# A gated attention and Mish block on one core: TensorE products on tiles of 64x32 in two fixed sets, with halves linked through SyncE

## The chip, the core and the metric

The kernel runs on one core of a Trainium2 chip. Five engines work side by side, each on its own queue in order: TensorE (PE in the profile; its weight loads are listed as PEld), VectorE (DVE), ScalarE (ACT), GpSimd (POOL) and SyncE (SP), which here issues nearly all DMAs. They wait for each other through semaphores. The metric is the device time of one execution in microseconds; the kernel before took 746.05 us (median of three runs, 746.04 to 746.26).

## What is computed

`x` is 2048 tokens of 640 channels in bf16. Two branches are mixed by a gate of one number per token:

```python
g = sigmoid((x * gate_w).sum(-1, keepdims=True))
qkv = x @ wqkv                                  # 32 heads of 20 channels
p = softmax(q @ k.T * 20 ** -0.5)               # 32 x 2048 x 2048
a = (p @ v) @ wo
h = x @ w1 + b1                                 # 1536 channels
b = (h * tanh(softplus(h))) @ w2                # Mish
out = g * a + (1 - g) * b
```

The bulk is the exponential of 32 x 2048 x 2048 scores, which have to leave PSUM (TensorE's output memory, 8 banks of 128 x 512 f32) through ACT or DVE.

## The kernel before

**Attention.** The heads are taken four at a time (8 quads p), the queries 512 at a time (4 chunks c), in 32 groups of 64 score units (`uinfo`, line 396). A unit is one head, one block of 128 keys and 512 queries: one matmul of 32 rows (20 channels, zero padded) by 128 keys, on one of four row strips of the array (`emit_score`, line 933), into one PSUM bank. Up to four units of different heads are issued together and use the four strips at once. Seven banks (`NBANK`) hold scores and every other product; the eighth (`ACCB`) holds the attention output of the current group.

**Exponential.** A unit is read either by ACT (line 1312, one instruction for one, two or three adjacent banks) into a ring of 34 bf16 buffers `E`, or by DVE (line 1347), which writes the bits of a bf16 number by a multiply and an add in integers. To make that piecewise-linear exponential good, three shifted copies of it are summed: two more copies are made from the first with an integer add by POOL or DVE (line 1365, two units per instruction). So an ACT unit is one operand for the product with the values and a DVE unit is three.

**Values.** The product with V takes 128 keys by 32 columns per matmul, on one of four column strips (`emit_pv`, line 1000): four heads run at once and add up in bank `ACCB`. DVE copies the finished group out (line 1406); the softmax denominator, which a column of ones in V delivers, makes a round trip through DRAM over SP's queue (`acc_out`, lines 1592 to 1631), and POOL multiplies.

**The rest of TensorE's work** is cut in pieces of one contraction step each ("misc" units: projections of q, k and v, the dense layer and its second product, the output projection). Each piece is four matmuls of 128 rows by 32 columns on the four column strips (`mm4`, line 512).

**Order.** Python code (`make_plan`, line 422) walks through a clock with costs, and decides what each engine's next instruction is: `poll_pe` (line 1156) prefers scores, then value products, then misc pieces by due times. A constant `ORDER` (line 124) then gives the order in which the planned steps are put into the program. PE takes its queue in that order; an instruction that waits holds everything behind it. Between matmuls on row strips (32x128) and matmuls on column strips (128x32) the plan charges 111 ns (`pe_run`, line 893).

```python
    def emit_score(n, bk):
        g, p, c, kt, r = uinfo(n)
...
                K.kT[32 * r : 32 * r + 32, p % 3, kt * P : (kt + 1) * P],
                K.qT[32 * r : 32 * r + 32, p % 3, c * QC : (c + 1) * QC],
...
                (32 * r, 0),
```

Of the kernel before, what the change touches and what calls it, by code (L numbers as in the profile page):

```python
# [11 lines left out]
P = 128  # L12
ACT = mybir.ActivationFunctionType
ALU = mybir.AluOpType
# [9 lines left out]
VS = 22  # L24
# [28 lines left out]
for _c in range(NQC):  # L53
# [5 lines left out]
PAR = {  # L59
    "thr": 311.432865850951,  # L60
    "lead": 183.56579879480037,
    "dvw": 38.53743660585776,
    "gpmax": 3438.021927551807,
    "xmin": 2062.5527122350004,
    "xwait": 370.8568233744456,
    "urgent": 22.685657497992203,
    "kq": 2.9970653505716234,
    "v0": 30.539278203984722,
    "slack": 141.97275980676932,
    "fill": 0.64,  # L70
# [5 lines left out]
    "wl": 6.4206626210236575,  # L76
    "last": 2.936423220458476,
    "mb": 9,
    "elow": 20.682307524088536,
    "ahd": 5.108513768085364,  # L80
    "age": 6.220859528764049,
    "eres": 0.018977235113313735,
    "vk": 3,
    "a3": 7,
    "a3gp": 1688.8815596232141,
    "hold": 6,
    "idlek": 7,
    "swait": 155.25662470383708,
    "flush": 8,
    "tailh": 0,  # L90
    "dahead": 387.7453029112783,
    "mgb": 0.0,
    "xb": 3.0,
    "ph": 591.0767712730124,
    "wp": 37.52540751652794,
    "wo": 23.808422394577885,
    "thr_2": 337.7597040015291,
    "lead_2": 105.70712187325442,
    "gpmax_2": 6725.390524273934,
    "xmin_2": 3714.088827176782,  # L100
    "xwait_2": 515.3394389040967,
    "vk_2": 3.0,
    "a3gp_2": 2139.6517249172894,
    "dahead_2": 194.37405724273543,
    "age_2": 10.493975161462359,
    "ahd_2": 3.0816465538756317,
    "hold_2": 4.0,
    "idlek_2": 4.0,
    "mb_2": 8.0,
    "dvw_2": 36.65964931310165,  # L110
    "slack_2": 120.90571614233303,
    "mgb_2": 0.0,
# [4 lines left out]
for _k in ("thr", "lead", "gpmax", "xmin", "xwait", "vk", "a3gp", "dahead", "age", "ahd", "hold", "idlek", "mb", "dvw", "slack", "mgb", "xb"):  # L117
# [6 lines left out]
ORDER = (  # L124
    "007000000000000000000000000000000000000000005000000000000000000000000000000000000000000000000000000000000000000000000000001000"
    "000000000000000000000000000001000000002001000000000000000000000000001000000000000000000000001000000000000001000000000000001000"
    "000000000000000000000000000000000001000000000000000000000000000001000000000000000000000000000000000000000000000000000000000000"
    "000000000000000000000000000000000000000000000000000000000000000000000000001000000000000000000000000000000000000000000000000000"
    "000001000000000000000000000000000000000000000000000001000000000000000000001002000000001002000000000000000000000000000001000000"
    "000000000000000000000000000000000000000000000000000000000000000000000000000000000000000000000000000000000000000001004005006007"  # L130
    "00900800a00000000a00b00000000000000000100300000000d00000400100200300500600700800a00e009000002000002001000001000000003004006002"
    "00500700800000900b00a00c00d00e00800f01001301401601501201701901801101b01c01e01d01f00000600800700900a00b00c00d00e00f010016014013"
    "01201501a00000800a00000500000a00000200000200000000d000001003002000002001000000003001000004003000006001000006002003005007001000"
    "00500000200500b00000200000200400000600500700200900a00800d00c00b01000e01301101601201501701800f01901b01a01d01c01e01f020021023024"
    "02202502702802a02902c02f02e02b03003703503403303103a03603803903b02d03c03d04003f041042032044053000033032031000022023025027024029"
    "02802a02b02c02e02f03003103203303403803700002101d02302202402502602702802d02a03003102c00002402d02a03002e029031026039033032034035"
    "03600002e02f03403503203703603803903300002a02d02c03002e02f02103303103503a03403203c00002002102200000e01001400000100600500800400b"
    "00700c00300e00a00901001200d00f01501101300000300400500600800700900b00a00c00d00e01201001100001401101201301501901601b00000a01200b"
    "01301100f00000700800000600800900b00a00700d00c00e01001100f01201500000300400000500000400500900e00301000000500600800000000200000c"
    "00300600500b00e00a00900800700f01c01101001201301401601701501901801b01d01f01a01e00001401301a01901801501b016017000000000000000000"  # L140
    "00000100300700500800000a00c00800900b00400000d00b00c00f00500000400800000300000400300e00800900600a00700b01600d01000f011000000001"
    "00000000300200700600900000800900000a00500300600000700000300600100a00200800400f000005002007009000008000000000000001000000000000"
    "00500200000000100000100200000000100000200100000000100000100000100000100000000600100800400000900100a00500800c00300701001300b000"
    "00100000000000000200300900600a00b00c00d00e00101001101301401500000301300101501601b01701400e00401801901a01201c000012013000000001"
    "00300600800000c00800500200a00b00701001100d00e01401500f01301601701801a01201c01d01902702001b02202402301f02502802601e02a02102c02d"
    "02e03002f03202903403503703303803603a03b03c03102b03e03f03904104004404604504704804a04c04e04204d03d04f04905105204b043054053057056"
    "05005905505800005905805a05c05705d06305f06005b06205e06506106406706806a06606906d06c06f06e07007207107507707607307807d07a07c07f079"
    "08208106b08008408508308708807b08a08908b08608e09008d09209409308c08f07409609500009609109409209307809509c09809909a09d0970a309b000"
    "01701300000600500c00000f00700900a00601100801600d01201300c01701801000101f01501b01a01401c02401e02000001400000800a00c00d00e00f000"
    "00c000000000000000001008000000000005003002001006000003002006001004000003004000000000000000000000001000006009001005008002004007"  # L150
    "00d00c00b00e01100a01201301401900f00001300000700800000600700500800900b00a00d00e00c000001000002000003002004006009005019007000002"
    "00400600500300800900700d00a00e00f01401200000100800a00b00c00f00501000e00d00000300800200100500700600d00900f00a01000c00000700e00a"
    "00d01000f012011013000003000000000002001000000001000000000001000000000000000000001000000000000000000000000000000000000000002001"
    "00000100000000000100300400600000300600000000100400200300000000300100200400600a00800c00900500b00d00000b00700800d00a000003005007"
    "006000000002001000000000000000000000001002005003004000001000001000002001003000004000005002004006007000007000002001000000001000"
    "00000000000100200300500400a00900800700d00c00e00600f01101201001601401501701801a01e01b01301c01d02002301f02201902100001901c01a01e"
    "01d02001f02300000600701400900a00c00d00f00e01000b01600000200800100400000400300500100600900700a008000000002006003001005007008009"
    "00a00e00b00c00d01000f01101701201301601901801a01b00001b01a00000800900c00f01100e00d010000012011015016014013017018000000000000000"
    "00100200500400300600700d00c00b01100e00801000f01201301401601501b01702001a01801c01f01d01e02101902302400902502202602802702902c02b"
    "02d02e03002f03103302a00002a02b02e02d03003203303102c00000c00e00f00d01101001301400000e01301100000700b00c00a00501000400d000000001"  # L160
    "00000000000100300500000200600800700500900b00a00c00e00f01000d01201101501401601800001501601700000900000800700a00900600c00b00d010"
    "00f00e01100000000200000000200100300000100000200b00000200300500400700600800e00d00b00c00f00901101201501301401601701901801b01a01d"
    "01c02102001e01f02302502202602400001801701901c01b01e01d02200000500600700902c00a00d00c01400000400600500300800700a00b00c01300e00d"
    "01001401201101500000700000000000100000100300200f00500700001d00500600701000900002300602500002200d00400500e01002d00000100000601b"
    "00200901c00b00100001200700a00001e00700900601602d00b02302401801701902601b02502803402902a02b00c00a01d02c03a01203002e01f02f03c022"
    "02000002900702b01f00000001b00001701501801d01601c01a01e01f02102302202002402602802502700001801902001a01c01d01e01f021022023025024"
    "00000f00c00d00e01001101601201301401501701b01c01901a01802501d01f02302002202602401e02802102702902a02f02b03402e03102c02d030032036"
    "03803503304003c03a03904403b03d03e00003403b03703803a03c04103d02c04204000000e00800d01201301101601700901501400f010000000005001004"
# [85 lines left out]
    "00000b00000500700200900600000900a000000000004005000000002000000000"  # L254
)


class Names:
    pass


def unpack(text):

    lo, out = 0, set()
# [1541 lines left out]
```

## Time and profile before

| | |
|---|---|
| time, median of three runs | 746.05 us |
| the profiled execution, first to last instruction | 745.1 us |
| what lies around it | 0.95 us |
| TensorE clock granted | 1.000 |
| first score starts / last score starts | 10.4 us / 731.7 us |
| ACT: first exponential starts | 10.87 us |
| PE: matmuls, each with a weight load | 10,332 |
| score units read by ACT / by DVE | 1,464 / 584 |

How to read the profile: its page gives the busy time of each engine (matmuls are pipelined and their ends are modelled, so "busy" on PE is not PE at its peak), then the chain of work that ended last, then groups of like instructions, with busy time, mean duration of one, and the idle time just before them with what ended it. A group's mean duration contains the latency of an instruction (an ACT exponential of two banks lasts 1,060 ns but the next one starts 904 ns after it), so what an engine can carry is read from start to start.

### The profile page before, as it was taken

Reading aid. Unit: us, or ns where it says so; the run is one execution under the profiler, and the core shown is the slowest. Engines: PE = TensorE matmul, PEld = TensorE weight load, DVE = VectorE, ACT = ScalarE, POOL = GpSimd, SP = SyncE. Lnnn points to the kernel's source line nnn. Section 1 sums busy time; section 2 is a strip of 40 time slices with the busy share of each in tenths; the row PEclk is TensorE's granted clock in tenths of the full one; section 3 lists DMA queues with packets and bytes.
Section 4 is the critical chain, followed back from the end, with each engine's and each line's share of the span. In section 5 each row is a group of like instructions: output and inputs, shape, how many; then the busy total and the mean of one; then the engine's idle time right before and its main releaser. Section 6 shows DMA issues by size and latency. Waiting matters only on the chain.

```text
span 745.1 us, 24873 instructions
## 1 busy us (share of the span) xinstructions
PE 729.6 (98%) x10332; PEld 255.2 (34%) x10332; DVE 607.1 (81%) x1047; ACT 713.2 (96%) x750; POOL 521.9 (70%) x501
## 2 busy tenths in 40 slices
PE   8999999999999999999999999999999999999997
PEld 4433343333235333333332222223433333333333
DVE  4688888888979797988788878887878788797876
ACT  6899989999999999999999999999999999999995
POOL 9466735565578557667676587687986788797884
PEclk9999999999999999999999999999999999999999
DMA  9611120011011000112102211130111111211202
GB/s 284 199 48 54 50 82 17 20 52 39 17 29 60 16 29 26 50 44 74 39 28 59 54 43 50 39 101 21 43 52 39 39 38 39 71 60 60 72 21 86
DMA packets 45720, 41.82 MB, mean 56 GB/s; under 512 B 20120, under 2 KB 39240, under 8 KB 45608
## 3 DMA queue, kind: packets, MB, share of 16 engines
q1 hardware_dynamic: 42984, 39.94, 17.8%
q8 instruction: 80, 1.31, 0.7%
q10 hardware_dynamic: 2624, 0.31, 0.3%
q14 instruction: 32, 0.26, 0.1%
HBM read 27.59 MB, written 12.38 MB: 54 GB/s over the span
## 4 chain that ended last, share of the span: by engine, by line
PE 80%; ACT 10%; DVE 7%; issue 2%; POOL 0%; DVEq 0%; ACTq 0%; POOLq 0%
PE ps L507 80%; ACT E L1312 9%; DVE E L1347 4%; DVE E L1365 2%; DVE accs L1406 0%; POOL E L1365 0%; ACT act L1236 0%; PE ps L1753 0%; PE ps L520 0%; ACT xT L528 0%; ACT L1236 0%; DVE bst L656 0%; DVEq L1801 0%; DVE qT L544 0%; DVE ost L689 0%
## 5 line engine op out<-in xcount | busy, mean ns | idle before, releaser
L1312 ACT ACTIVATE E<-ps 128x1024 bf16<-128x1024 f32 (+2 forms) x723 | 680.0, 1070 | 19.3 <-PE ps L507 16.4
L1365 POOL TENSOR_SCALAR E<-E 128x1024 uint16<-128x1024 uint16 x431 | 457.8, 1063 | 209.7 <-DVE E L1347 155.0
L1347 DVE TENSOR_SCALAR E<-ps 128x512 uint16<-128x512 f32 x584 | 388.8, 684 | 94.1 <-PE ps L507 85.6
L507 PE MATMUL ps<-E,VA 128*32 128x512 bf16 x3216 | 299.4, 383 | 1.7 <-DVE E L1347 0.6
L507 PE MATMUL ps<-qT,kT 32*128 32x512 bf16 x2048 | 284.0, 384 | 5.3 <-ACT E L1312 2.6
L507 PEld LDWEIGHTS <-kT 32*128 32x128 bf16 x2048 | 75.3, 91 | 261.3 <-issue 257.2
L507 PEld LDWEIGHTS <-VA 128*32 128x32 bf16 x3216 | 78.9, 95 | 97.5 <-issue 78.2
L1365 DVE TENSOR_SCALAR E<-E 128x1024 uint16<-128x1024 uint16 x153 | 97.9, 643 | 2.0
L507 PE MATMUL ps<-R,act 128*32 128x320 bf16 x1536 | 87.1, 302 | 0.4 <-ACT act L1236 0.4
L507 PE MATMUL ps<-xT,R 128*32 128x512 bf16 x960 | 82.4, 383 | 0.0
L507 PEld LDWEIGHTS <-R 128*32 128x32 bf16 (+1 forms) x1728 | 40.8, 95 | 44.7 <-issue 34.0
L507 PEld LDWEIGHTS <-act 128*32 128x32 bf16 x1536 | 36.4, 95 | 32.1 <-issue 22.2
L637 DVE TENSOR_SCALAR act<-ps,b1f 128x512 bf16<-128x512 f32 x48 | 35.7, 744 | 7.4 <-PE ps L507 6.6
L507 PE MATMUL ps<-wv,xT 128*32 128x241 bf16 (+2 forms) x720 | 37.6, 276 | 0.5 <-DVE E L1347 0.3
L507 PE MATMUL ps<-wk,R 128*32 128x320 bf16 (+1 forms) x640 | 37.5, 303 | 0.2
L507 PE MATMUL ps<-xT,wq 128*32 128x512 bf16 x400 | 34.8, 383 | 0.1
L507 PE MATMUL ps<-xT,wk 128*32 128x512 bf16 (+1 forms) x360 | 34.7, 384 | 0.0
L1620 POOL TENSOR_TENSOR ons<-accs,rb 128x512 bf16<-128x512 f32 x24 | 31.5, 1310 | 1.8 <-DVE E L1347 0.7
L567 DVE CAST stg<-ps 128x512 bf16<-128x512 f32 (+1 forms) x40 | 27.3, 683 | 5.1 <-PE ps L507 4.9
L507 PEld LDWEIGHTS <-xT 128*32 128x32 bf16 (+1 forms) x720 | 19.6, 96 | 13.0 <-issue 9.4
L1406 DVE COPY accs<-ps 128x512 f32<-128x512 f32 x31 | 21.2, 684 | 1.3 <-PE ps L507 1.0
L1236 ACT ACTIVATE act<-act 128x3072 bf16<-128x3072 bf16 x8 | 21.5, 2752 | 0.0
(72 smaller groups left out, 190.3 us busy)
## 6 DMA issues: line engine op xcount, KB each, us to landing
rb<-rd_d SPq DMA_DIRECT2D x124, 64.0 KB
qd<-stg SPq DMA_DIRECT2D x20, 128.0 KB
b_d<-bst SPq DMA_DIRECT2D x16, 160.0 KB
out_dram<-ost SPq DMA_DIRECT2D x16, 160.0 KB
kT<-kd SPq DMA_DIRECT2D x28, 80.0 KB
qT<-qd SPq DMA_DIRECT2D x28, 80.0 KB
stg<-b_d SPq DMA_DIRECT2D x13, 160.0 KB
kd<-stg SPq DMA_DIRECT2D x16, 128.0 KB
```

The costliest lines, as they stand in the source:

```text
L507: K.nc.tensor.matmul(o, lhsT=l, rhs=r, start=first, stop=last, tile_position=pos, skip_group_check=True)
L567: K.nc.vector.tensor_copy(out=K.stg[0:w, s, :], in_=bank(b)[0:w, :])
L637: K.nc.vector.tensor_scalar(out=K.act[:, f, (c % 2) * QC : (c % 2 + 1) * QC], in0=bank(b), scalar1=K.b1f[:, f : f + 1], scalar2=None, op0= ...
L1236: K.nc.scalar.activation(a, a, ACT.Mish)
L1312: lambda: K.nc.scalar.activation(K.E[:, e : e + w, :], K.ps[:, b0 : b0 + w, :], ACT.Exp, scale=SCALE)
L1347: lambda: K.nc.vector.tensor_scalar(out=K.E[:, e + h, :].bitcast(U16), in0=K.ps[:, b, :], scalar1=CH_MUL, scalar2=CH_OFF + CH_ADD[0], op0= ...
L1365: eng.tensor_scalar(out=o, in0=i, scalar1=float(CH_ADD[k]), scalar2=1.0, op0=ALU.add, op1=ALU.mult)
L1406: emit(lambda: K.nc.vector.tensor_copy(out=K.accs[:, g % 2, :], in_=K.ps[:, ACCB, :]))
L1620: gp_q.append((1350.0, lambda: K.nc.gpsimd.tensor_tensor(out=dst(), in0=K.accs[:, b, :], in1=K.rb[:, b, :], op=ALU.mult), lambda: pl.give( ...
```

## The change

Every product in the steady part uses tiles of 64 rows by 32 columns, of which the array has eight. They are divided in two fixed sets of four: set 0 is the tiles (row 0, columns 0 and 32) and (row 64, columns 64 and 96), set 1 the other four.

- **Scores** run on set 1. A unit is now 64 keys of two heads: four matmuls of 64 rows by 32 keys by 512 queries (rows of two heads at once; q is kept twice, with the rows of the one or of the other head zero, by a mask). 32 key blocks times two head pairs give 64 units per group, 2,048 in all, as before. Units are issued one at a time (`try_score`).
- **Values** run on set 0. A unit's 128 rows are 64 keys of one head and 64 of another, so each operand takes two matmuls on two tiles; two operands fill the set.
- **Misc pieces** are contracted in two halves of 64 rows: one half of a unit runs all its pieces on one set, then the other half on the other set, into the same bank. Between the halves stands a link: an empty SyncE instruction that waits for the first half's last matmul, and for which the second half's first weight load waits.
- The gate's sums become a unit of their own (`add_z`). The layout of V, k and q changes to fit; k and q have two buffers in place of three. SP steps of several DMAs are issued DMA by DMA in the plan. Filler matmuls (112 before) go.
- The plan's parameters are others, and the planned order is used as it stands (`ORDER` goes).

```diff
+    def row_of(side, q):
+        return q // 2 if side == 0 else 1 - q // 2
+
+    def mmh(side, o, l, r, first, last, cols=P):
+        for q in range((cols + 31) // 32):
+            w, a = min(32, cols - 32 * q), 64 * row_of(side, q)
+            mm(o[32 * q : 32 * q + w, :], l[a : a + 64, 32 * q : 32 * q + w], r[a : a + 64], first, last, (a, 32 * q))
...
     def add_blk(which, j, c, due):
-        def pc(kt, b):
+        def pc(kt, b, row, first, last):
-            mm4(bank(b), W[:, kt, c0 : c0 + w], K.xT[:, kt, c * QC : (c + 1) * QC], kt == 0, kt == KT - 1, w)
+            mmh(row, bank(b), W[:, kt, c0 : c0 + w], K.xT[:, kt, c * QC : (c + 1) * QC], first, last, w)
...
+    def link(key, op):
+        def fn():
+            K.nop = K.nc.sync.nop()
+            K.tc.add_manual_dep(K.nop.ins, K.lastmm[key].ins.name, K.sync, reason="row tiles in turn")
+        emit(fn)
+        want[0] = False
+        i = len(pl.ops)
+        pl.run("SP", 20.0, dep=(op,), kind="link")
+        return (i,)
+
+    def link_ok(start):
+        if pl.t < start + par["link"]:
+            pl.at(start + par["link"], lambda: None)
+            return False
+        if pl.free["SP"] > pl.t + 1e-6:
+            want[0] = True
+            return False
+        return True
...
     def emit_score(n, bk):
-        g, p, c, kt, r = uinfo(n)
-            mm(
-                K.ps[:, bk, :],
-                K.kT[32 * r : 32 * r + 32, p % 3, kt * P : (kt + 1) * P],
-                K.qT[32 * r : 32 * r + 32, p % 3, c * QC : (c + 1) * QC],
...
+        g, p, c, _, h = uinfo(n)
+        t = n % 64 // 2 * 64
+            for q in range(4):
+                a, k = 64 * row_of(1, q), t + 32 * (q % 2)
+                mm(K.ps[32 * q : 32 * q + 32, bk, :], K.kT[a : a + 64, p % 2, k : k + 32],
+                   K.qT[a : a + 64, p % 2, h, c * QC : (c + 1) * QC], True, True, (a, 32 * q))
...
     def emit_pv(g, items):
-                mm(K.ps[32 * r : 32 * r + 32, ACCB, :], K.VA[:, kt, h * VS : h * VS + 32], ap(), first, fin, (0, 32 * r))
+                o = j * 16 * VS + x * VS
+                for i in range(2):
+                    a, q = 64 * i, 2 * i + h
+                    mm(K.ps[32 * q : 32 * q + 32, ACCB, :], K.VA[a : a + 64, o : o + 32], ap()[a : a + 64], first, fin, (a, 32 * q))
...
+        if m.i == n and md == "H" and m.phase == 0:
+            m.i, m.phase, m.row = 0, 1, 1 - m.row
...
     plan = make_plan(K, PAR)
-    for i in unpack(ORDER):
-        for fn in plan["pl"].fns[i]:
+    for fns in plan["pl"].fns:
+        for fn in fns:
             fn()
```

Instructions of the two built programs, where they differ most:

| | before | after |
|---|---|---|
| score matmuls | 2,048 (32x128) | 8,192 (64x32) |
| value matmuls | 3,216 (128x32) | 6,816 (64x32) |
| matmuls in all, each with a weight load | 10,332 | 27,044 |
| ACT exponentials of one / two / three banks | 15 / 675 / 33 | 873 / 231 / 11 |
| units read by DVE | 584 | 680 |
| copies by DVE / by POOL | 153 / 431 | 166 / 514 |
| links on SP | 0 | 177 |
| DMAs issued by SP | 566 | 566 |

More of the change, by code (lines that the diff above doesn't have):

```diff
@@ L258 @@
 class Names:
     pass
-def unpack(text):
-    lo, out = 0, set()
-    for k in range(0, len(text), 3):
-        i = lo + int(text[k : k + 3], 16)
-        yield i
-        out.add(i)
-        while lo in out:
-            out.remove(lo)
-            lo += 1
 class Misc:
@@ L279, in __init__ @@
         self.i = 0
+        self.row, self.phase, self.last, self.left = None, 0, None, 1
 class Clock:
@@ L291, in __init__ @@
         self.free = {e: 0.0 for e in self.LAT}
+        self.free.update(P0=0.0, P1=0.0)
+        self.tile = [[0.0] * 4 for _ in range(2)]
+        self.mode, self.pend_end = None, 0.0
         self.tok = set()
@@ L456, in ldn @@
     def ldn(fs):
[L457 to L462 removed]
+        return [ld(f) for f in fs]
     for (a, b), t in zip(XD, XAT):
@@ L506, in mm @@
     def mm(o, l, r, first, last, pos):
-        K.nc.tensor.matmul(o, lhsT=l, rhs=r, start=first, stop=last, tile_position=pos, skip_group_check=True)
+        i = K.nc.tensor.matmul(o, lhsT=l, rhs=r, start=first, stop=last, tile_position=pos, skip_group_check=True)
+        if K.nop is not None:
+            K.tc.add_manual_dep(i.ins, K.nop.ins.name, K.sync, reason="row tiles in turn")
+            K.nop = None
+        K.mm = i
+    def row_of(side, q):
[4 more added lines that the diff above has]
+            mm(o[32 * q : 32 * q + w, :], l[a : a + 64, 32 * q : 32 * q + w], r[a : a + 64], first, last, (a, 32 * q))
     def mm1(o, l, r, first, last):
@@ new lines, in pc @@
+        def pc(i, kt, b, side=None, first=None, last=None):
+            for q in range(4):
+                if side is None:
+                    prod(i, kt, b, q, 0, P, kt == 0, kt == KT - 1)
+                else:
+                    a = 64 * row_of(side, q)
+                    prod(i, kt, b, q, a, a + 64, first, last)
+        def ev(b):
+            K.nc.vector.tensor_copy(
+                out=K.VAv[:, 2 * t0 : 2 * t0 + nb, 2 * p0 : 2 * (p0 + np_), 0:DH],
+                in_=bank(b)[:, 0 : nb * w].rearrange("p (b h d) -> p b h d", b=nb, d=DH),
+            )
@@ L1091, in run_piece, with other, both @@
                 done = lambda: act_q.append((620.0, lambda: m.evac(m.bank), lambda: misc_done(m)))
+            elif m.name == "q0.0":
+                m.left = 2
+                def other():
+                    K.nc.scalar.activation(K.qT[:, 0, 1, 0:QC], bank(b), ACT.Copy, scale=K.mask[:, 1:2])
+                def both():
+                    dve_q.append(("misc", m))
+                    act_q.append((620.0, other, lambda: misc_done(m)))
+                done = both
             else:
                 done = lambda: dve_q.append(("misc", m))
-        pe_run(md, dur, done, wr=[("b", b)], dep=dep, kind="M" + m.name)
+        rows = (m.row,) if md == "H" else range(2)
+        cols = range(4) if md != "H" or not m.name.startswith("kb4") else range(2)
+        i, start = pl.run_pe(rows, cols, dur, done, md=md, wr=[("b", b)], dep=dep, kind="M" + m.name)
+        m.last = (i, start)
+        if m.i == n and md == "H" and m.phase == 0:
+            m.i, m.phase, m.row = 0, 1, 1 - m.row
         return True
     def misc_done(m):
+        m.left -= 1
+        if m.left:
+            return
         free_b.add(m.bank)
```

673 lines of the change are left out of this document (305 added, 368 removed).

## The prediction

> **What bounds the kernel now.** I read the page's busy times, its clock row and its chain first:
>
> ```profile
> span 745.1 us, 24873 instructions
> ...
> PE 729.6 (98%) x10332; PEld 255.2 (34%) x10332; DVE 607.1 (81%) x1047; ACT 713.2 (96%) x750; POOL 521.9 (70%) x501
> ...
> PEclk9999999999999999999999999999999999999999
> ...
> PE 80%; ACT 10%; DVE 7%; issue 2%; POOL 0%; DVEq 0%; ACTq 0%; POOLq 0%
> ```
>
> PE and ACT are both full, the clock is full, and the chain runs over PE. What fills PE shows in a timeline of PE, 1.5 us from the middle:
>
> ```profile
> 301.50 0.39 PE L507 MATMUL ps<-qT,kT 32*128 32x512 bf16 x3
> 301.82 0.83 PE L507 MATMUL ps<-E,VA 128*32 128x512 bf16 x12
> 302.59 0.39 PE L507 MATMUL ps<-qT,kT 32*128 32x512 bf16 x3
> ```
>
> Twelve value matmuls (three rounds of four) start at 301.82, and the next scores start 0.77 us later. A round in such a row starts 216 ns after the last one, so three are 0.65 us and 0.1 us is left. Three scores take 0.32 us until the values start, where one round is 0.216. So each turn between row strips and column strips costs about 105 ns. In the order of the built program the tiling changes 1,401 times: 147 us of PE. The rest of PE, counted in rounds (216 ns for 512 columns, 136 for 320, the rows of such rounds in the trace), is 496 us, so 643 in all.
>
> ACT is tighter. The groups by form:
>
> ```profile
> L1312 ACT ACTIVATE E<-ps 128x1024 bf16<-128x1024 f32 x675 | 632.1, 1060 | 16.1 <-PE ps L507 13.4 <-POOL E L1365 0.5 <-ACT E L1312 0.3
> L1365 POOL TENSOR_SCALAR E<-E 128x1024 uint16<-128x1024 uint16 x431 | 457.8, 1063 | 209.7 <-DVE E L1347 155.0 <-PE ps L507 19.3 <-ACT E L1312 6.6
> L1347 DVE TENSOR_SCALAR E<-ps 128x512 uint16<-128x512 f32 x584 | 388.8, 684 | 94.1 <-PE ps L507 85.6 <-ACT E L1312 2.3 <-issue 0.6
> L1312 ACT ACTIVATE E<-ps 128x1536 bf16<-128x1536 f32 x33 | 48.8, 1478 | 0.8 <-PE ps L507 0.6
> L1312 ACT ACTIVATE E<-ps 128x512 bf16<-128x512 f32 x15 | 9.4, 628 | 2.5 <-PE ps L507 2.4
> ```
>
> From start to start without a gap, ACT takes 904 ns for two banks, 1,330 for three and 476 (shortest) to 501 (median of 8) for one. At 478 for one bank, the exponentials are 675 x 0.904 + 33 x 1.330 + 15 x 0.478 = 661.3 us; their starts really cover 696.4, so ACT waits 35.1: 16.6 in gaps behind PE, and 18.5 that hide in the pace. **The sum of the run on ACT**: 10.9 to the first exponential, 661.3 + 35.1, 27.4 of other ACT work (Mish 21.5, table loads), 10.4 of tail = 745.1. The median of the runs lies 0.95 above. DVE idles 134.8 us in all, 85.6 of it waiting for scores.
>
> **The change, part by part.**
>
> *Turns between tilings go.* 147 us of PE disappear, apart from 47 turns at the start and end (5 us). PE's total is then no longer one number: set 1 carries 2,048 units x 0.216 = 442 us of scores and 191 of misc halves, set 0 carries 6,816 / 4 x 0.216 = 368 of values and 191 of halves; 18 of full-array work at the ends stand on both. That is 651 and 577 us, beside each other. That tiles of 64x32 keep the 216 ns per round the trace doesn't show; rows of 128x32 rounds give 216 (226 after a turn). I take 216, and leave 226 in the range: +10 ns x some 3,050 rounds = 30 us on set 1.
>
> *ACT.* 873 x 0.478 + 231 x 0.904 + 11 x 1.330 = 640.8, 20.5 less than before: 96 units more go to DVE, but most units go one bank at a time, and 392 launches more pay 51 ns each (2 x 478 - 904). At 501 per single it would be 660.9, no gain: this end stays in the range. A copy of q adds 0.6.
>
> *DVE and POOL.* 96 more reads at 0.637 (starts of this group without gaps, 372 us over 584) and 13 more copies at 0.59, less some 3 us for fewer V copies: 610 + 66 = 676 us. POOL's 83 further copies at 1.008 (shortest start to start) make 525 + 84 = 609. Both fit, but DVE has 60 us left instead of 135.
>
> *Where ACT isn't the longest.* I cut both built programs in 16 stretches of 128 units and priced each engine by these rows. Before, ACT is longest in all 16. After, ACT needs 39 to 42 us in 13 of them (the others hold the first start or Mish), set 1 29 to 42 and DVE 34 to 44 in the same 13. In six DVE or set 1 is longer, by 14 us together, 11 of it in the first two stretches. This is added.
>
> *ACT's waits.* The 16.6 us of gaps behind PE come where scores stand behind turns and misc rounds; one unit at a time without turns should halve that: 8. The 18.5 in the pace I keep. Bounds: nothing, if the banks' slack covers all; 70, twice the old waits, as PE, ACT and DVE are now nearly equal and each wait passes on.
>
> *Links.* 177 of them. PE takes its queue in order, so a weight load that waits for SP holds both sets, and with them ACT and DVE as soon as the filled banks are read. The link stands in SP's queue behind DMAs; the plan places it where SP is free by its own costs, 432 ns after the first half's last start (a matmul lasts 383). How far SP runs late is seen in the timeline of SP and the DMA view of the same place:
>
> ```profile
> 137.49 3.43 SPq L1599 DMA_DIRECT2D den<-accs  x4
> ```
>
> ```profile
> q8 instruction: 1, 0.02, 4.1%
> ```
>
> Four such issues take 2.5 us elsewhere (0.59 each, 0.64 apart); here the fourth took 1.6, and in that window one 16 KB fetch of PE's instructions ran. 22 of the issues after 40 us exceed 0.9 us, nearly all beside one of the 80 fetches of q8. With 54,083 PE rows in place of 20,659 there are some 210 fetches: 58 long issues, about 1 us each, 8% of the run. A link that meets one waits some 0.5 us: 177 x 0.08 x 0.5 = 7. I take 5, as filled banks cover part; the bounds are 0 and 53 (every link meets half an issue of 0.59).
>
> *Moved or neutral.* The DMAs are the same 566. The gate's sums add 640 short matmuls, inside the 191. Filler matmuls (112, 6 us of PE) go; the clock stays granted, since both sets stream longer than PE does now. The masks and memsets lie before 10.4 us, beside the loads of x: nothing, or 1 us without that cover.
>
> **Sum**: 10.9 + 640.8 + 28.0 + 10.4 = 690.1; + 14 + 26.5 waits + 5 links = 735.6; + 0.95 = **736.6 us**, 1.3% under 746.05.
>
> **A rule that speaks against it.** In the row of rounds above, the loads for the next four tiles start 13 ns after the first of the running ones, while those stream. The Trainium skill, "TensorE: Matmul & The Clock Gate", section "Part 3: Packing small matmuls", says that weight loads overlap running matmuls only when the row group differs (or when they go to the background buffer). Taken alone, its first half would forbid what the trace shows for 128x32; for 64x32 no run here shows it yet.
>
> **Rivals.**
>
> 1. *The waits go altogether*: gaps and surplus are taken up by the banks, as scores come singly. 690.1 + 18.5 + 1 + 0.95 = 711. For it: PE loses its turns. Against it: three engines near 40 us per stretch, and some five of the seven banks for scores.
> 2. *The links hold PE* (slower). Place: the weight load after a link. Price: 177 x the mean hold. SP is in an instruction 273 of 745 us, 0.37 of the time; 0.37 x half of 0.45 us, plus 0.08 x 0.5 for fetches, is 0.12 us, 22 in all, up to 53 in the bounds; with the old waits kept whole (+9) 763, up to 794. It decides from about 0.08 us per link, where the gain of 9.5 us and the 5 already counted are used up. For it: no other engine's lateness can pass SP, and SP waits 137 us for `rden`, 111 for `ons`, 79 for `accs`, wherever DVE or POOL run behind the plan. Against it: most of those waits are planned.
> 3. *Loads don't overlap in a row group of 64*: each round waits for its loads, 92 ns (the mean of a load), so 3,050 rounds x 0.092 = 281 us more on set 1, which then needs 932: some 955.
> 4. *The two sets don't run side by side*, so the change doesn't do what it says: 442 + 368 + 382 + 18 = 1,210.
>
> **Chances.** Forecast 0.36 (725 to 744), rival 1 0.16, no difference 0.06, rival 2, and the dearer single or round with it, 0.35, rival 3 0.04, rival 4 0.03. Within 0.2% of 746.05 a measurement can't tell this kernel from no change, so that is "same". Faster 0.52, same 0.06, slower 0.42. The range, 711 to 790, reaches rival 1's time and nearly rival 2's bound, takes in ACT's dearer single (+20) and the slower round (+30), and leaves out rivals 3 and 4. As both signs hold much of it: the likeliest case alone spans 725 to 744.
>
> **What would show it.** Rounds of 64x32 216 ns apart within a set, and starts of the two sets interleaved; if loads of a set start only when its matmuls end, rival 3. ACT's group of 128x512 near 478 from start to start, its waits behind PE near 8 us. PE's waits for SP: a sum under 10 us bears the forecast out, over 20 rival 2. SP issues over 0.9 us: some 60. The forecast is wrong if DVE or the score set, not ACT, sets the pace in the middle stretches: then ACT shows idle time behind PE everywhere, not in places.

## The result and the profile after

The changed kernel takes 864.24 us (median of four runs, 861.03 to 866.32) beside 746.15 us for the kernel before: 1.157 times as long, with a 95% interval of 1.154 to 1.161. The forecast was 736.6 us, and the time lies far outside the range of 711 to 790. The profiled execution took 862.34 us, its span 860.6.

The page of the changed kernel: busy times, the slices of PE and of its clock, queue q8, and the chain.

```profile
span 860.6 us, 59674 instructions
...
PE 765.9 (89%) x27044; PEld 502.4 (58%) x27044; DVE 677.7 (79%) x1134; ACT 714.4 (83%) x1143; POOL 616.0 (72%) x585
...
PE   7666777999999898889999999999999987898996
...
PEclk8998699999999999999999999999999999999998
...
q8 instruction: 211, 3.46, 1.7%
...
PE 68%; issue 12%; DVE 9%; DMA 4%; ACT 3%; SPq 2%; POOL 1%; POOLq 0%; ACTq 0%; DVEq 0%
```

No engine is full any more, and "issue" (time in which an engine waited for nothing that the profile shows) has grown from 2% of the chain to 12%. PE's slices show where: the first sixth of the run, the middle at places, and the last sixth. The waits of the same kernel (who waited for whom: us in total, times, the longest):

```profile
PEld L425 <- issue: 192.8, 398, 4.7
POOL E L1357 <- DVE E L1339: 175.8, 108, 25.7
ACT E L1301 <- PE ps L425: 111.4, 111, 8.2
DVE E L1339 <- PE ps L425: 83.1, 118, 6.9
PE ps L425 <- issue: 68.0, 76, 4.6
...
PEld L425 <- SPq L850: 10.1, 25, 1.2
...
PE ps L425 <- SPq L850: 1.9, 4, 0.7
```

ACT's exponentials wait 111.4 us for PE (16.4 before), and PE's matmuls wait 68 us for "issue", up to 4.6 us at a time. The links, which stand as SPq, hold PE for 12.0 us in all. What a wait for "issue" looks like, in PE's timeline (start, duration, instruction, and in brackets the idle time before it):

```profile
75.35 0.46 PE L425 MATMUL ps<-wv,xT 64*32 64x1 bf16 x25
75.64 0.41 PE L425 MATMUL ps<-qT,kT 64*32 64x512 bf16 x4
75.68 0.24 PE L425 MATMUL ps<-wv,xT 64*32 64x1 bf16 x9
77.91 0.19 PE L425 MATMUL ps<-wv,xT 64*32 64x1 bf16 x5 [1.86 <-issue]
...
79.17 0.31 PE L425 MATMUL ps<-wv,xT 64*32 64x1 bf16 x13
81.37 0.30 PE L425 MATMUL ps<-wv,xT 64*32 64x1 bf16 x17 [1.75 <-issue]
```

Short matmuls of the z unit run, PE stops for 1.9 us though the profile shows nothing that it waits for, runs again for 1.5 us, stops again. The trace's records of queue q8, which brings PE's instructions in packets of 16 KB, have packets that end at 76.66 and 80.07 us: PE resumes 1.3 us after each. It had run out of instructions: stretch B of the run with PE alone, below, has the same picture with nothing else in it. In this kernel 154 gaps of over 0.4 us between the starts of PE's matmuls add up to 142 us, and 84 us of that lie in gaps that end 1.25 to 1.5 us after such a packet.

The 211 packets hold 54,088 rows (a matmul is one row, its weight load another), 256 to a packet. Their starts are never less than 3.26 us apart; the quarter of the intervals that is shortest lies under 3.57, the median is 3.77. In the kernel before the shortest interval was 5.1 us and the median 9.2. Cut by the score units as in the prediction, with the rows of each stretch priced at 71 per us, the pace that PE alone got (below):

| stretch of 128 score units | rows after | rows / 71 per us | us after | us before |
|---|---|---|---|---|
| 1 | 6,535 | 92 | 102.7 | 49.7 |
| 4 | 2,571 | 36 | 41.9 | 44.4 |
| 6 | 3,766 | 53 | 53.0 | 45.1 |
| 10 | 2,055 | 29 | 40.4 | 43.9 |
| 14 | 4,584 | 65 | 68.7 | 41.2 |

Where the rows ask for more than some 42 us at 71 per us, the stretch takes that long or longer (by 11 us in the first). Where they ask for less, the changed kernel is the faster one in six of eight stretches and the slower one in two, 11 (43.9 us against 42.1) and 13 (44.0 against 42.0). In stretches 3, 4 and 8 to 11 together it needs 254.3 us against 263.6, 3.5% less; the work beside the scores isn't spread over the stretches alike in the two kernels, so this is only a rough comparison.

**Theory 1**: PE's instructions arrive at no more than one block of 256 rows per some 3.5 us, 71 to 73 rows per us, and this sets the end. **Theory 2** (rival 2 of the prediction): the links on SP hold PE. **Theory 3**: the two sets hold each other up on the array or in PE's one queue.

### The profile page after: what moved, and what is told of

Same layout as the page of the kernel before. It is cut to its first block, busy times and chain, and to the rows that moved or that the text cites. A ratio compares the mean times of both kernels' runs of the same rounds, so it can differ in the third digit from the quotient of the medians.

```text
span 860.6 us, 59674 instructions
## 1 busy us (share of the span) xinstructions
PE 765.9 (89%) x27044; PEld 502.4 (58%) x27044; DVE 677.7 (79%) x1134; ACT 714.4 (83%) x1143; POOL 616.0 (72%) x585
## 4 chain that ended last, share of the span: by engine, by line
PE 68%; issue 12%; DVE 9%; DMA 4%; ACT 3%; SPq 2%; POOL 1%; POOLq 0%; ACTq 0%; DVEq 0%
PE ps L425 67%; DVE E L1339 6%; ACT E L1301 3%; SPq L375 2%; DVE E L1357 2%; DMA den<-accs 1%; POOL E L1357 1%; DMA wq<-in_A_wqkv_dram 1%; DMA stg<-b_d 0%; DMA wk<-in_A_wo_dram 0%; DMA rb<-rd_d 0%; PE ps L451 0%; DMA rd_d<-rden 0%; DVE act L589 0%; ACT act L1224 0%
## 5 line engine op out<-in xcount | busy, mean ns | idle before, releaser
L1301 ACT ACTIVATE E<-ps 128x512 bf16<-128x512 f32 (+2 forms) x1115 | 680.4, 737 | 126.9 <-PE ps L425 111.4
L1357 POOL TENSOR_SCALAR E<-E 128x1024 uint16<-128x1024 uint16 x514 | 551.0, 1075 | 224.9 <-DVE E L1339 175.8
L425 PE MATMUL ps<-qT,kT 64*32 64x512 bf16 x8192 | 604.8, 379 | 17.4 <-issue 9.4
L425 PE MATMUL ps<-E,VA 64*32 64x512 bf16 x6816 | 529.3, 380 | 13.5 <-issue 9.5
L425 PEld LDWEIGHTS <-kT 64*32 64x32 bf16 x8192 | 262.1, 91 | 137.4 <-issue 65.1
L425 PEld LDWEIGHTS <-VA 64*32 64x32 bf16 x6816 | 193.0, 91 | 65.1 <-issue 41.7
L425 PE MATMUL ps<-xT,R 64*32 64x512 bf16 x1920 | 150.6, 377 | 2.0 <-SPq L850 1.3
L425 PE MATMUL ps<-R,act 64*32 64x320 bf16 x3072 | 144.1, 297 | 6.9 <-issue 5.6
L425 PE MATMUL ps<-wv,xT 64*32 64x120 bf16 (+3 forms) x3840 | 90.9, 209 | 35.1 <-issue 34.7
L425 PEld LDWEIGHTS <-R 64*32 64x32 bf16 (+1 forms) x3392 | 86.6, 92 | 37.3 <-issue 14.5
L589 DVE TENSOR_SCALAR act<-ps,b1f 128x512 bf16<-128x512 f32 x48 | 35.6, 741 | 2.9 <-PE ps L425 2.7
```

Of the source, the lines that this page charges most:

```text
L425: i = K.nc.tensor.matmul(o, lhsT=l, rhs=r, start=first, stop=last, tile_position=pos, skip_group_check=True)
L589: K.nc.vector.tensor_scalar(out=K.act[:, f, (c % 2) * QC : (c % 2 + 1) * QC], in0=bank(b), scalar1=K.b1f[:, f : f + 1], scalar2=None, op0= ...
L1301: lambda: K.nc.scalar.activation(K.E[:, e : e + w, :], K.ps[:, b0 : b0 + w, :], ACT.Exp, scale=SCALE)
L1357: eng.tensor_scalar(out=o, in0=i, scalar1=float(CH_ADD[k]), scalar2=1.0, op0=ALU.add, op1=ALU.mult)
```

## Experiments

### PE alone

A kernel of PE products only (it leaves out the whole block and writes zeros), in stretches: A, 500 rounds on all eight tiles of 64x32, 512 columns; B, the same with 64 columns; C, 300 rounds with set 0 in 64x32 and set 1 in two tiles of 64x64; D, four tiles of 64x64; E, set 0 alone; F, as E with three more weight loads ahead of each matmul; G, as B while SP issues 60 small transfers.

```diff
+    rounds(500, 512)
+    rounds(500, 64, 2, 3)
+    for k in range(300):
+        for p in SET0:
+            mm(4, p, 32, 512, k)
+        for p in BIG1:
+            mm(5, p, 64, 512, k)
...
```

> TensorE's products alone; nothing of the reference is computed and the output is zeros. Stretches in order: A, 500 rounds of eight 64x32 tiles of 512 columns (8,000 PE rows); B, the same with 64 columns; C, 300 rounds with set 0 in 64x32 and set 1 in 64x64; D, four tiles of 64x64; E, one set of 64x32 alone; F, as E with three more weight loads per matmul; G, as B while SP issues 60 small transfers. Theory 1 (PE's instructions can't be fetched faster than 256 rows in some 3.4 us): A runs at its 216 ns per round or just above it (16 rows per 0.216 us is 74 rows per us, 3.46 us per 256 rows), B is held to about 75 rows per us or less, so 500 rounds take some 105 us where the array needs about 15, and the fetches of q8 stand 3.3 to 3.5 us apart in B and G. Theory 2 (the two sets hold each other up in order): A is slower than E per round; B isn't held, under 40 us. C and D tell whether 64x64 tiles beside 64x32 tiles cost turns: 216 ns per round if not, some 430 if each round pays two turns of 105.

Stretches A and B by windows (length, busy time and count on each engine, granted clock):

```profile
14.70:126.90 112.20, 110.60 (x4015) 63.37 (x4000) 0.00 (x0) 0.00 (x0) 1.00 0.02 5
126.90:239.80 112.90, 39.84 (x4001) 35.77 (x4001) 0.00 (x0) 0.00 (x0) 0.52 0.02 4
```

PE's timeline in B:

```profile
155.33 1.27 PE L35 MATMUL ps<-w 64*32 64x64 bf16 x128 [2.45 <-issue]
158.78 1.27 PE L35 MATMUL ps<-w 64*32 64x64 bf16 x128 [2.18 <-issue]
```

Here PE starts the 256 rows of one packet within 1.05 us, even at half its clock, and then stands until 1.25 to 1.6 us after the next packet has ended. So it isn't PE's own pace that limits B. At each of its 30 stops there it has started 256 k + 447 rows, where k is the number of the packet that it waits for, counted from 0; in the changed kernel's timeline above, both stops come at that same count.

A and B take nearly the same time for the same 8,000 rows, 71 per us, though B moves an eighth of the columns: PE is busy for a third of B. No other engine takes part, and both have 31 packets, a median of 3.51 us apart. In A the median round takes 216 ns and the mean 224, since here and there a block is late: two sets of 64x32 at full pace ask for 74 rows per us, just over the supply. G gave 69 rows per us, so the small transfers cost little. D and E gave 216 ns per round, D with half as many rows for the same use of the array. C took 660 ns per round where some 430 had been expected: it is two rounds of 216 in a row and two turns of 114, so a set of another tile width doesn't run beside the first. F took 492 ns, so each further load into one tile costs (492 - 216) / 3 = 92 ns.

### Fewer rows through wider tiles

The first try at fewer rows in the real kernel used tiles of 64x64: for scores and dense halves, for scores alone, for dense halves alone (values stay at 64x32).

```diff
-            for q in range(4):
-                a, k = 64 * row_of(1, q), t + 32 * (q % 2)
+            for q in range(2):
+                a = 64 * row_of(1, 2 * q)
...
-                    (a, 32 * q),
+                    (a, 64 * q),
```

> The kernel after with the same plan, and scores and misc halves on tiles of 64x64 in place of two of 64x32; values stay on 64x32. PE rows fall from 54,083 to 34,771, array time, links, waits and all other engines' instructions stay. Theory 1 (instruction fetch): 136 fetches, 470 us of them in all, so PE stalls only in the densest places: 735 to 765 us, PE's idle on issue from 260 us under 60. Theory 2 (the links and SP): no change, 855 to 870. Theory 3 (two sets in one queue in order): no change, 855 to 870. If tiles of 64x64 beside 64x32 cost a turn each, above 1,000.

> The kernel after with only the scores on 64x64 tiles: 45,891 PE rows, 179 fetches. Theory 1: between after and the run with both, about 805 us, as the densest stretch, between 15 and 160 us, is made of misc pieces with few columns and keeps most of its rows. Theories 2 and 3: 855 to 870.

> The kernel after with only the misc halves on 64x64 tiles: 42,963 PE rows, 168 fetches. Theory 1: more gain than from the scores, about 775 us, since the short pieces are what asks for most rows per us. Theories 2 and 3: 855 to 870.

They took 1463.27 us (1.959 times the kernel before, 1.952 to 1.965), 1520.43 us (2.034, 2.026 to 2.042) and 1187.16 us (1.588, 1.581 to 1.595). PE's timeline in the first:

```profile
399.77 0.39 PE L425 MATMUL ps<-E,VA 64*32 64x512 bf16 x2
400.09 0.40 PE L425 MATMUL ps<-qT,kT 64*64 64x512 bf16 x2
400.42 0.39 PE L425 MATMUL ps<-E,VA 64*32 64x512 bf16 x2
```

Values and scores start 0.32 us after each other, one round and a turn, where the changed kernel starts them 0.02 us apart. So as tests of theory 1 these runs say nothing: the turns hide whatever the rows gain. They show that a set of 64x64 tiles doesn't run beside a set of 64x32. The next edits keep one width. A kernel with all its products on 64x64, which D would allow, wasn't tried.

### The same rows with less array time, and the reverse

Two edits of the changed kernel leave nearly the same columns to the array. In the first, every product of the dense halves moves a quarter of its columns (all that go through `mmh`; the value projections don't).

```diff
-            mm(o[32 * q : 32 * q + w, :], l[a : a + 64, 32 * q : 32 * q + w], r[a : a + 64], first, last, (a, 32 * q))
+            n = max(1, r.shape[-1] // 4)
+            mm(o[32 * q : 32 * q + w, 0:n], l[a : a + 64, 32 * q : 32 * q + w], r[a : a + 64, 0:n], first, last, (a, 32 * q))
```

> The changed kernel with every matmul of the projections and dense units moving a quarter of its columns (the other columns of those results are left out). Instructions, links and plan are the same: 54,083 PE rows; the columns moved fall from 11.36 to 8.96 million (21 per cent less array time). Theory 1 (PE's instructions come in blocks of 256 rows at one per some 3.5 us, about 71 rows per us): rows set the time, so 835 to 866 us. Theory 2 (the links on SP hold PE): the same links, 850 to 866 us. Theory 3 (the two sets hold each other up on the array in one in-order queue): less array time, so well below, 700 to 790 us.

In the second, the contraction pieces between the first and the last are left out.

```diff
-            emit(lambda: fn(b, row, first, last))
-            keep(key)
+            k = m.i % KT if m.name[0] == "v" else m.i
+            if m.i in (0, n - 1) or (m.name[0] == "v" and k in (0, KT - 1)) or m.name == "z":
+                emit(lambda: fn(b, row, first, last))
+                keep(key)
```

> The changed kernel with only the first and last contraction piece of each half of the projections, hidden and output units issued (the pieces between are left out of the sums); plan, links (394 of 397) and evictions as they were. 39,972 PE rows; 8.98 million columns, as many as with quarter columns. Theory 1: 39,972 / 71 = 563 us on the average, under the ScalarE sum of 690, so PE is no longer held: 715 to 770 us, about what was forecast for the change. Theory 2: the links are all there, so 850 to 866 us. Theory 3: the same array time as with quarter columns, so the same time as that run.

With a quarter of the columns: 862.93 us (1.154 times before, 1.149 to 1.158), as slow as the changed kernel. With fewer pieces: 784.35 us (1.049, 1.046 to 1.052). The columns are the same within 0.2%, and so are the links within a few (the 397 and 394 of the expectations count all of SP's waits; 177 of them are links in both plans), so the 79 us between them go with the rows, some 14,100 fewer in the second. Theories 2 and 3 fall as the main cause. Theory 1 was off in size for the second: it gave 715 to 770. What is left lies in the first stretch, 91.0 us, where the value and z units still stand close; from the second on this run needs 664.7 us to the last score, against 671.6 in the kernel before.

### More rows in the kernel before

Here nothing of the change is present. Each matmul of 256 columns or more is issued as two, or as three, over parts of its columns with the same weights. (The start flag is set on every part, so sums over several pieces aren't those of the reference.)

```diff
-        K.nc.tensor.matmul(o, lhsT=l, rhs=r, start=first, stop=last, tile_position=pos, skip_group_check=True)
+        n = r.shape[-1]
+        cut = [n * i // 2 for i in range(3)] if len(r.shape) == 2 and n >= 256 else [0, n]
+        for x, y in zip(cut, cut[1:]):
+            K.nc.tensor.matmul(o[:, x:y], lhsT=l, rhs=r[:, x:y], start=first, stop=last, tile_position=pos, skip_group_check=True)
```

> The kernel before with each matmul of 256 or more columns issued as two over half the columns each, same weights, same plan: no links, no sets of tiles, the same columns moved, 40,300 PE rows in place of 20,660. Theory 1: 40,300 / 71 = 568 us on the average, but a stretch may go over the rate: 746 to 800 us. Theories 2 and 3: what they name isn't there; 746 to 755 us.

> The same in three parts: 59,940 PE rows, the same columns moved. Theory 1: at least 59,940 / 71 = 844 us, 850 to 950 us. Theories 2 and 3: 746 to 765 us.

Two parts: 764.22 us (1.022, 1.019 to 1.025), within what theory 1 gave and over the 755 of the others. Three parts: 914.75 us (1.223, 1.218 to 1.227). The page of the run with three:

```profile
span 915.7 us, 64298 instructions
...
PE 818.4 (89%) x29972; PEld 592.4 (65%) x29972; DVE 614.5 (67%) x1047; ACT 745.5 (81%) x750; POOL 520.7 (57%) x501
...
q8 instruction: 234, 3.83, 1.8%
...
PE 84%; issue 10%; DVE 3%; ACT 2%; DMA 0%; POOL 0%; DVEq 0%; ACTq 0%; POOLq 0%
```

It looks like the changed kernel: no engine full, PE at 89%, a tenth of the chain on issue, packets a median of 3.75 us apart. The step from 40,304 to 59,944 rows costs 150 us with the same columns and no link in the program, and the average demand passes the supply between the two: 40,304 rows ask for 568 us, 59,944 for 844. The gaps of over 0.4 us between the starts of PE's matmuls add up to 118 us (24 in the kernel before), and 97 us of that lie in gaps that end 1.2 to 1.5 us after a packet. A rival for a part of it: thirds of a value product start 77 ns after each other (median), 231 ns for three where a whole round takes 216. On the 496 us of rounds of the prediction that would be some 35 us, an estimate, which no run separates from the rest.

### Where the rows stand close

If the loss is local, rows taken out of the dense first stretch should give it back nearly one to one. Most of the contraction of z and of the linked value projections is left out, with everything else as in the changed kernel; then the same (and the first value projections) is added to the run with two pieces.

```diff
+                if kt % 4:
+                    continue
                 l = K.xT[:, kt, t * P : (t + 1) * P]
...
-            emit(lambda: fn(b, row, first, last))
-            keep(key)
+            if m.name[0] != "v" or m.i in (0, n - 1) or m.i % KT == 0:
+                emit(lambda: fn(b, row, first, last))
+                keep(key)
```

> The changed kernel with most of the contraction of the z unit and of the linked value projections left out (one or two of five pieces stay): 2,240 matmuls, 4,480 PE rows fewer of 54,090, but only 2.3 per cent of the columns, and all 397 links stay. About 880 of these matmuls lie in the first 128 scores. Theory 1 (rows, block by block where they are dense): 1,760 rows / 71 = 25 us less there, up to 14 us less in the next 128 scores and little later: 805 to 840 us. Theory 2 (links): 850 to 866 us. Theory 3 (array time): at most 2.3 per cent of 766 us less, 845 to 866 us.

> The run with only the first and last contraction pieces, and most of the contraction of all value projections and of z left out too: 37,800 PE rows, 394 links. Theory 1: the loss that was left in the run with two pieces lies in its first 128 scores (91.0 us against 49.7), where some 1,536 of 2,792 matmuls are of these units; about 900 matmuls go there, 1,800 rows / 71 = 25 us: 745 to 768 us from 784. From the second 128 scores on it should be even with the kernel before or some 1 per cent faster. Theory 2: as the run with two pieces, 780 to 786 us or more. Theory 3: the columns are nearly the same (8.92 against 8.98 million), so 778 to 786 us.

The first took 813.67 us (1.090, 1.086 to 1.094). The first stretch fell from 102.7 to 79.2 us (23.5, expected 25), the second from 57.5 to 46.8; stretches 5 to 7 gave another 17.6, where the last value units stand and little had been expected. Not all of the 23.5 need be rows: PE's clock is half for 27 us of the changed kernel's first stretch, and for 10 us of it here. The second took 756.63 us (1.013, 1.009 to 1.018), its first stretch 61.2 us. Its waits:

```profile
PEld L425 <- issue: 263.8, 864, 1.7
...
DVE E L1343 <- PE ps L425: 32.4, 70, 2.0
ACT E L1305 <- PE ps L425: 28.2, 43, 1.8
PEld L425 <- SPq L852: 15.5, 33, 1.3
...
PE ps L425 <- SPq L852: 4.3, 8, 1.2
```

The waits of matmuls for issue are down from 68.0 to 3.8 us; what remains for issue are weight loads, which the kernel before has too (422.3 us there). ACT's waits for PE are down from 111.4 to 28.2 us, with all other work as in the changed kernel. From the second stretch on it needs 667.1 us, 0.7% less than the kernel before.

### The whole computation with fewer rows

These two kernels do the whole computation. In the first, the value projections and the z unit are contracted over 128 rows at once, on 128x64 tiles or the whole array, their pieces in clumps; plan rules and parameters are the changed kernel's.

```diff
-                mmh(side, bank(b)[:, t : t + 1], l, K.wv[:, kt, V0 : V0 + 1], first and kt == 0, last and kt == KT - 1)
+                mm1(bank(b)[:, t : t + 1], l, K.wv[:, kt, V0 : V0 + 1], kt == 0, kt == KT - 1)
...
+            for q in range(2):
+                o = bank(b)[64 * q : 64 * q + 64, i * w : (i + 1) * w].rearrange("p (q x) -> p q x", x=40)
+                mm(o, K.xT[:, kt, t : t + 64], r[:, :, h : h + 40], kt == 0, kt == KT - 1, (0, 64 * q))
```

> One part of the change undone, with the whole computation: the value projections and the z unit are contracted over 128 rows at once, on two tiles of 128x64 or on the whole array (their pieces issued up to 1.15 us in a row), in place of eight 64x32 matmuls in two linked halves. 24,228 matmuls in place of 27,044 (48,452 PE rows, 5,636 fewer), 152 links in place of 177, and 92 changes of tiling in place of 47 (45 x 105 ns = 5 us more). The plan's parameters and rules are the changed kernel's; its own clock ends 11 us later. Theory 1: at most 5,636 / 71 = 79 us less, at least the 50 us that leaving out much of the same units gave: 785 to 825 us. Theory 2: 25 of 177 links fewer are 14 per cent of what links cost; even if they cost all of the 118 us lost, 847 us or more. Theory 3: the same array time and more turns: 860 us or more.

In the second, the plan knows the supply, and its parameters are searched anew.

```diff
+        while self.blk >= 0 and r0 >= 256 * self.blk + 200:
+            self.last = max(self.last + 3520.0, at)
+            self.fd.append(self.last + 2500.0)
+            self.blk += 1
+        k = (r0 - 447) // 256
+        if k >= 0:
+            at = max(at, self.fd[k])
```

> The same (and the first projection on the whole array), with the whole computation, and with a plan that knows the supply: a block of 256 rows can be fetched 3.5 us after the last at the earliest and when all but some 56 rows of the block before have gone, is there 2.5 us later, and PE runs dry one block on. The plan's parameters were searched anew with that rule; its own clock ends at 730.4 us (the changed kernel's, without the rule, at 736.1, and at 823 with it). 48,430 PE rows, 152 links. Theory 1: no stretch is over the rate any more, so about the plan's end and the 10 to 20 us that the run with both cuts lay above its plan: 735 to 770 us; under 746 it would beat both kernels. Theory 2: the links stay, 830 us or more. Theory 3: the array time stays and turns are added, 850 us or more.

The first took 808.03 us (1.084, 1.078 to 1.090), within what theory 1 gave. The second took 781.78 us (1.044, 1.040 to 1.048): 82 us under the changed kernel with the same mathematics, but 12 over the upper end expected of it, and slower than the kernel before. Its waits:

```profile
PEld L443 <- issue: 116.2, 351, 2.9
...
ACT E L1329 <- PE ps L443: 50.2, 90, 2.0
DVE E L1367 <- PE ps L443: 40.6, 83, 1.8
PEld L443 <- SPq L877: 27.8, 64, 1.6
...
PE ps L443 <- SPq L877: 7.8, 12, 1.1
PE ps L443 <- issue: 7.7, 14, 2.4
```

Waits of matmuls for issue are 7.7 us in place of 68, so the plan's rule did its work. The links now hold PE for 35.6 us in place of 12.0, probably since a PE that isn't starved arrives at them earlier; the plan is another too, so this isn't shown. PE still has 58 us in 80 gaps of over 0.4 us, and a block still comes every 3.86 us in the median. How much of the 51 us above the plan's own end belongs to links, and how much to a supply that is asked for 87% of its most (682 of 782 us), wasn't separated. No version was found that beats the kernel before.

## Why the prediction was wrong

**The step that failed** is in the part on links: "With 54,083 PE rows in place of 20,659 there are some 210 fetches: 58 long issues, about 1 us each, 8%". The count was right (211), and it was priced only by what a fetch does to SP's issues. What fetches can bring to PE itself had no price and no bound. At one per 3.5 us, 211 of them are some 738 us (762 at 71 rows per us), already more than the forecast with all its waits, and clumps make it worse: 6,535 rows, 92 us of supply, stand in the first stretch, which took 49.7 us in the kernel before. The view that showed it was the one used: the queue's row gave 80 packets before, and the trace had none closer than 5.1 us. The highest supply that the kernel before ever showed was thus 256 / 5.1 = 50 rows per us, while the forecast needed 54,083 / 736.6 = 73 as a mean. That is a resource used beyond anything the trace shows, and it should have been bounded from both sides like the others.

The Trainium skill, "Runtime: NRT & Kernel Launch", section "Instruction fetch mechanics", says that instructions come in blocks of 256, and that fetching is hidden because engines issue more slowly than the blocks arrive. The trace agrees on the blocks (256 rows per packet) and, for the kernel before, on the hiding; at 71 rows per us it doesn't hold: in stretch B above PE starts a packet's rows in 1.05 us and waits 2.4 us for the next. By that rule the extra rows would have cost nothing; an estimate of the time by it is the 756.6 us of the run with both cuts, and the measurement of 864 decides.

Point by point:

- *Turns go, 64x32 keeps its pace, the sets run side by side*: right. PE's timeline of the changed kernel:

```profile
400.01 0.39 PE L425 MATMUL ps<-E,VA 64*32 64x512 bf16 x4
400.02 0.39 PE L425 MATMUL ps<-qT,kT 64*32 64x512 bf16 x4
400.22 0.39 PE L425 MATMUL ps<-E,VA 64*32 64x512 bf16 x4
400.24 0.39 PE L425 MATMUL ps<-qT,kT 64*32 64x512 bf16 x4
```

  Both sets start a round every 0.21 to 0.22 us, 0.01 to 0.02 apart. The quoted half of the Trainium skill's rule on weight loads ("TensorE: Matmul & The Clock Gate", section "Part 3: Packing small matmuls") is too strict for these tiles: one set of 64x32 alone keeps 216 ns per round with a load before every matmul, and since halves of 256 columns take 109 ns in the kernel before (median, issued as two), 512 columns leave no room for a load of 92 ns between rounds. Rivals 3 and 4 are out.
- *ACT's singles at 478 ns*: right, 477 to 478 in the median of those without a gap.
- *ACT's waits, 8 us of gaps behind PE*: 111.4 in the changed kernel, the loss itself; 28.2 with the rows cut.
- *Links, 5 us, rival 2 at 22 and more*: PE waits 12.0 us for SP, between the two signs that were named. Long SP issues are 44, not 58. But where PE isn't starved the waits are 19.8 and 35.6 us, so the 5 was too low, and rival 2's price of 22 the better one. The result lies on the slower side for another reason than rival 2, beyond its bound of 794.
- *The start, and the clock that stays granted*: the first score started at 14.7 us in place of 10.4 (11.1 to 12.4 in four runs with the same plan), so this term was some 4 us too low here. The clock was half for 34 of the first 103 us, and full from there to 853.8 us. What the halved clock adds to the first stretch wasn't separated from the rows.
- *DVE, POOL and where ACT isn't longest*: the sums were near (DVE busy 677.7 us for 676, POOL 616.0 for 609), and not what decided. With the rows cut the changed kernel comes to 756.6 us. So some 108 of the 128 us between forecast and result went with the rows that those cuts take out; the cuts take array time too (21% of the columns), but the run with a quarter of the columns shows that this alone gives nothing.

## What to carry to other kernels

Count instructions per microsecond on TensorE, not only columns: halving a tile and halving a contraction each double the rows, and a plan whose every product fits may still ask for more rows than arrive. Compare the demand, as a mean and for each stretch, with the shortest interval between packets of the instruction queue that any trace of the chip shows, and treat a demand beyond it as unknown. Clumps of short products were the dearest here: the 4,480 rows left out of the z unit and the value projections held 2.3% of the columns, and leaving them out gave back 51 us.

## What the runs showed of the hardware

- A packet of 256 PE rows comes no more often than every 3.25 us (the shortest interval in any of these runs), and PE that lives on them alone gets 71 rows per us. Why a packet takes that long stays open.
- PE has one block in hand, no more. At the start of packet k (counted from 0) it has started some 256 k + 200 rows where it isn't held (174 to 236 more than 256 k in the kernel before, from the third packet on); where it is starved, as in stretch B, 256 k + 438 to 447 after the first packet of the stretch. So quiet stretches save up no more than some 250 rows for a dense one.
- A starved PE can lose its clock. The granted clock is half from 78.9 to 102.8 us of the changed kernel (the 6 in its slices), rounds are 0.43 us apart there, and in stretch B it is 0.52 in the mean. In stretch 14 of the changed kernel, which takes 68.7 us where its rows ask for 65, it stays full. In the run with both cuts it is full from 4.1 us to the end of the work.
- Tiles of 64x64 beside tiles of 64x32 cost a turn each way, 114 ns, though they share no part of the array; the 105 ns between row and column strips in the kernel before is of the same size. The Trainium skill, "TensorEngine Tiling (Array Packing)", section "Key Properties", says that changing the tiling mode drains TensorE, and the 114 and 105 ns agree with that.
